# A planner driven by events, and nine pairs of heads kept on the chip, in a two-level attention kernel with an MLP behind it

## The chip, the cores and the metric

The kernel runs on one core of a Trainium2 chip. The metric is the device time of one execution in microseconds (us); the time before is the median of three runs. Five engines work side by side, each through its own list of instructions in order: TensorE (PE, with its weight loads as PEld), VectorE (DVE), ScalarE (ACT), GpSimd (POOL) and SyncE (SP, which here only issues DMAs). Engines wait for one another by semaphores. A DMA is issued by SP, ACT or POOL and carried out by 16 DMA engines that all queues share.

## The reference

Eight batches of eight heads, 576 tokens, head size 64. Each head's output is the sum of two attentions; the result goes through an MLP with 2048 hidden units.

```python
q_d, k_d, v_d = means of q, k, v over groups of 4 tokens       # 144 coarse tokens
out_up = repeat(softmax(q_d @ k_d.T / 8) @ v_d, 4)             # coarse attention
mask = abs(pos_i - pos_j) < 4                                  # a band of 7 keys
out_local = softmax(where(mask, q @ k.T / 8, -1e9)) @ v        # local attention
x = (out_up + out_local) as [8 * 576 tokens, 8 * 64]
h = x @ w_in;  result = (h * sigmoid(h)) @ w_out
```

## The kernel before, in words

**Attention** goes by pairs of heads, 32 of them; four pairs are one batch, that is 576 rows of `x`. For a pair `p` the steps are:

- `load_qk`, `load_v` and `load_vq` fetch q and k, v in overlapping windows of 64 tokens (rows of 256 bytes), and for pairs from `NVP` = 8 on v a second time in groups of four tokens. `cast`, `castw` and `castv` turn them to bf16, mostly on POOL; `castv` also adds the groups of four up (pooled v, tile `vd`).
- `T(p)`: 36 transposes of 64x64 by TensorE; `after_T` moves them out of PSUM (`qT`, `kT`) and adds up groups of four with two reductions on VectorE (`qd`, `kd`).
- `S(p)`: the scores, 20 local and 8 coarse matmuls into the banks `AB`; `after_S` takes two exponentials on ScalarE (`Pt`, `Pd`) and multiplies the local one by the 0/1 band on VectorE.
- `Z(p)`: the row sums by TensorE into columns of the banks `CD`; `after_Z` takes the reciprocal (`zr`). For `p < NDIR` = 4 it is split into three bf16 parts and spread over partitions by 15 matmuls (`RB`). For all others it goes to DRAM (`scr`) and comes back spread out (`Rb`): three DMAs on ACT's queue, the last two of which wait for the first to land.
- `PV(p)`: the products with v and pooled v, in `CD`; `after_PV` multiplies by `Rb` on VectorE (`xo`) and adds the coarse to the local part on POOL into `xT`, a ring of 1536 tokens.
- For pairs under 8 pooled v comes by 14 matmuls (`VP`) instead of `load_vq`.

From pair 6 on these steps are packed into visits: `V(n)` is PV of pair n-2, S of n, T of n+1 and Z of n-1, in one unit of TensorE.

**The MLP** goes by nine blocks of 512 tokens. `g1(j, f)` is four matmuls for 128 of the 2048 hidden units, `tanh` on ScalarE and one operation on VectorE into `gT`; the two banks `HP` take turns. `g2(j, tt, part)` is a quarter of 16 matmuls for 128 tokens of output; after the fourth quarter ScalarE evicts and SP stores. Block j can start when all pairs of its tokens are in `xT`: block 0 needs pairs 0 to 3, block 1 pairs 4 to 7.

**The order** is written out by hand for the units (`T0 T1 S0 T2 S1 Z0 RB0 ...`, then two or three `g1` after each step, and from visit 10 on four `g1` and four `g2` per visit). `Plan.order` then goes through each engine's units in a window (14 units on PE, 30 on POOL, 40 elsewhere) with assumed costs, and takes the first that is ready. DMAs are modelled by a ring per issuing engine. The eight weight loads, 1 MB of DRAM each, are given to POOL's queue at 10, 14, 18, 22, 34, 38, 42 and 46 us of planned time. Each engine runs its list in that order whatever the real times are.

Of the kernel before, what the change touches and what calls it, by code (L numbers as in the profile page):

```python
# [1 line left out]

# [16 lines left out]
NVP = 8  # L19
NDIR = 4  # L20


class Res:


    def __init__(self, name, psum=False):
        self.name, self.psum = name, psum
        self.writers, self.readers, self.prev = [], [], []
        self.last = {}
        self.dw, self.dr, self.prev2, self.dl = [], [], [], {}  # L30
# [11 lines left out]
class Prog:  # L42
# [23 lines left out]
    def op(self, eng, fn, r=(), w=(), dma=None):  # L66
# [4 lines left out]
        for x in r:  # L71
            if x.psum:
                deps += [(o, False) for e, o in x.last.items() if e != eng]
            else:
                deps += [(o, True) for o in x.writers]
        for x in w:
            if x.psum:
                deps += [(o, False) for e, o in x.last.items() if e != eng]
# [70 lines left out]
class Unit:  # L149


    __slots__ = ("eng", "name", "ops", "cost", "dcost", "prio", "idx", "pre", "succ", "npre",
                 "ready", "start", "end")

    def __init__(self, eng, name, cost, prio, dcost=0.0):
        self.eng, self.name, self.cost, self.prio, self.dcost = eng, name, cost, prio, dcost
        self.ops, self.pre, self.succ = [], set(), []
        self.ready = 0.0


class Plan:


    LAT = {"PE": 0.25, "ACT": 0.2, "DVE": 0.2, "POOL": 0.2, "SP": 0.1}

    def __init__(self):
        self.units = []

    def unit(self, eng, name, cost, prio=None, dcost=0.0):
        u = Unit(eng, name, cost, prio, dcost)  # L170
        u.idx = len(self.units)
        if u.prio is None:
            u.prio = u.idx
        self.units.append(u)
        return u

    def op(self, u, fn, r=(), w=(), dma=None):
        u.ops.append((fn, tuple(r), tuple(w), dma))
        pre = set()
        for x in r:  # L180
            if x.psum:
                pre.update(x.dw)
                pre.update(v for v in x.dr if v.eng != u.eng)
                x.dr.append(u)
            else:
                pre.update(x.dw)
        for x in w:
            if x.psum:
                pre.update(x.dw)
                pre.update(x.dr)  # L190
                if x.dr or not x.dw or x.dw[-1] is not u:
                    x.dr, x.dw = [], [u]
            else:
                if x.dr or x in r:
                    x.prev2 = x.dr + x.dw
                    x.dr, x.dw = [], []
                pre.update(x.prev2)
                pre.update(v for v in x.dw if v.eng != u.eng)
        for x in r:
            if not x.psum and x not in w:  # L200
                x.dr.append(u)
        for x in w:
            if not x.psum:
                x.dw.append(u)
        pre.discard(u)
        u.pre |= pre

    def order(self, look):
        free = {e: 0.0 for e in Prog.ENGS}
        ring = {e: 0.0 for e in Prog.ENGS}  # L210
        for u in self.units:
            u.pre = {v for v in u.pre}
            u.npre = len(u.pre)
            for v in u.pre:
                v.succ.append(u)
        pend = {e: [u for u in self.units if u.eng == e] for e in Prog.ENGS}
        head = {e: 0 for e in Prog.ENGS}
        taken = set()
        res = []
        left = len(self.units)  # L220
        while left:
            best = None
            for e in Prog.ENGS:
                lst = pend[e]
                while head[e] < len(lst) and lst[head[e]] in taken:
                    head[e] += 1
                win = [u for u in lst[head[e]:head[e] + look[e]] if u not in taken and not u.npre]
                if not win:
                    continue
                t = max(free[e], min(u.ready for u in win))  # L230
                c = min((u for u in win if u.ready <= t + 0.05), key=lambda u: (u.prio, u.idx))
                t = max(t, c.ready)
                if best is None or t < best[0]:
                    best = (t, c)
            t, u = best
            u.start = t
            free[u.eng] = t + u.cost
            if u.dcost:
                e = u.eng
                begin = max(t + u.cost + 0.4, ring[e])  # L240
                other = max(x for y, x in ring.items() if y != e)
                ring[e] = begin + u.dcost + min(u.dcost, max(0.0, other - begin))
                u.end = ring[e] + 1.6
                if e == "SP":
                    free[e] = max(free[e], ring[e] - 4.0)
            else:
                u.end = t + u.cost + self.LAT[u.eng]
            for v in u.succ:
                v.npre -= 1
                same = v.eng == u.eng and not u.dcost  # L250
                v.ready = max(v.ready, t + u.cost + (0.06 if u.eng != "PE" else 0.0) if same else u.end)
            taken.add(u)
            res.append(u)
            left -= 1
        res.sort(key=lambda u: u.start)
        return res


def bass_hourglass_attn__then__act_silu_kernel(
# [9 lines left out]
    with kctx:  # L269
        E = kctx.enter_context  # L270
        L = Plan()
# [7 lines left out]
        def sb(name, shape, dt, n=1):  # L279
            ts = [E(nc.sbuf_tensor(f"{name}{i}", shape, dt)) for i in range(n)]  # L280
            return ts if n > 1 else ts[0]

        NQK, NVS, NVQ, NB, NX, NT, NP_, NV, NR = 4, 4, 2, 3, 2, 2, 4, 4, 3
        w_in_sb = sb("w_in_sb", [128, 4, DFF], F32R)
        w_out_bf = sb("w_out_bf", [128, 16, 512], BF16)
        xT = sb("xT", [128, 4, XR], F32)
# [3 lines left out]

        qk = sb("qk", [128, 2, 576], F32, NQK)
        vs = sb("vs", [128, 10, 64], F32, NVS)
        vq = sb("vq", [128, 4, 256], F32, NVQ)
        vt = sb("vt", [128, 4, 128], F32)
        qkb = sb("qkb", [128, 2, 576], BF16, NB)
        vb = sb("vb", [128, 10, 64], BF16, NV)
        vd = sb("vd", [128, 4, 64], BF16, NV)
# [4 lines left out]
        Pt = sb("Pt", [128, 2, 288], BF16, NP_)  # L302
        Pd = sb("Pd", [128, 2, 216], BF16, NP_)
        zr = sb("zr", [128, 2, 72], F32, 2)
        Rb = sb("Rb", [128, 720], F32, NR)
        xo = sb("xo", [128, 2, 360], F32, NX)
        scr = [nc.dram_tensor(f"scr{i}", [128, 144], F32, kind="Internal").ap() for i in range(NR)]

        sel = gT[1][:, 0:2, :].rearrange("p a (y m) -> p (a y) m", m=128)[:, 0:5, :]
        selr = [R("g1_0"), R("g1_1")]  # L310
# [43 lines left out]
        def constants():  # L354
# [13 lines left out]
            for i in range(NT):  # L368
                for a, b in ((0, 3), (579, 592)):
                    zero(kT[i][:, a:b], f"kTp{i}{a}", cost=0.07)  # L370
# [561 lines left out]
```

## Time and profile before

| | |
|---|---|
| three runs | 392.88 us median, 388.90 to 393.71 |
| span of the profiled execution | 389.9 us (no other time of it is given) |
| busy: PE / DVE / ACT / POOL | 337.1 / 239.5 / 169.1 / 159.1 us |
| moved by DMA | 66.1 MB, 170 GB/s over the span |
| one `g1` matmul, one `g2` matmul (mean) | 430 ns x576, 380 ns x546 |
| reciprocal of 128x144 | 1056 ns x32 |

How to read it: matmuls are pipelined, so 430 ns is the length of one and four in a row take 0.92 us. A busy PE is not a fast PE: the row PEclk tells the granted clock in tenths. A group's line gives its tile out and in, the line of the source, the count, the busy time, and the idle time of the engine before it with what ended it. L339 is the helper that records every matmul and L426 the one that records every DMA, so these are told apart by tile.

### The profile page before, as it was taken

How to read it: one execution, taken by the hardware profiler on the slowest of the kernel's cores; microseconds unless marked ns; L12 is line 12 of the kernel's file. 1: busy time of each engine (PE TensorE's matmuls, PEld its weight loads, DVE VectorE, ACT ScalarE, POOL GpSimd, SP SyncE). 2: the span in 40 equal slices, each digit the busy share in tenths (PEclk: the TensorE clock that was granted, in tenths of full speed). 3: DMA queues.
4: the chain of work that ended last, by engine and by line, in shares of the span. 5: the costliest groups of instructions: out<-in, count | busy, mean ns of one | idle time of the engine just before them, and what ended most of it. 6: DMA issues, size and time to landing. Idle time of an engine off the chain costs nothing.

```text
span 389.9 us, 12145 instructions
## 1 busy us (share of the span) xinstructions
PE 337.1 (86%) x5262; PEld 219.8 (56%) x5292; DVE 239.5 (61%) x395; ACT 169.1 (43%) x296; POOL 159.1 (41%) x199
## 2 busy tenths in 40 slices
PE   2587497545699998999989999899999999999996
PEld 1365265434466665656656666566665556656642
DVE  6686456555678867667868688677676443344310
ACT  3643245323255445545545455354553334344321
POOL 7371643435846564655556466555311200000000
PEclk9998668985599999999999999999999999999999
DMA  6999999996968896897797878443222201001012
GB/s 185 283 332 310 224 272 239 230 249 136 270 185 221 216 241 188 208 261 205 208 262 189 229 209 203 129 115 104 77 101 74 74 27 54 29 27 54 29 54 81
DMA packets 79038, 66.12 MB, mean 170 GB/s; under 512 B 47242, under 2 KB 60554, under 8 KB 78986
## 3 DMA queue, kind: packets, MB, share of 16 engines
q1 hardware_dynamic: 66250, 46.68, 45.2%
q10 hardware_dynamic: 8512, 12.39, 12.2%
q0 software_dynamic: 4224, 6.29, 6.7%
q8 instruction: 41, 0.67, 0.7%
q14 instruction: 11, 0.09, 0.1%
HBM read 55.93 MB, written 11.50 MB: 173 GB/s over the span
## 4 chain that ended last, share of the span: by engine, by line
PE 68%; DMA 15%; SPq 6%; issue 3%; DVE 3%; ACTq 2%; ACT 2%; POOL 1%; POOLq 0%; DVEq 0%
PE HP L339 32%; PE o L339 21%; DMA scr<-zr 10%; PE pe_ L339 7%; SPq L426 6%; PE CD L339 5%; DMA vs<-in_v_dram 4%; ACTq L426 2%; PE AB L339 2%; DMA Rb<-scr 1%; DVE gT L754 1%; PE o L531 1%; PE pe_ L531 1%; DVE zr L673 1%; ACT th L752 1%
## 5 line engine op out<-in xcount | busy, mean ns | idle before, releaser
L339 PE MATMUL HP<-xT,w_in_sb 128*128 128x512 f32 x576 | 167.7, 430 | 8.9 <-DVE gT L754 4.6
L754 DVE SCALAR_TENSOR_TENSOR gT<-th,HP 128x512 bf16<-128x512 f32 x144 | 96.7, 685 | 114.4 <-ACT th L752 114.1
L339 PEld LDWEIGHTS HP<-xT,w_in_sb 128*128 128x128 f32 x576 | 109.7, 196 | 39.0 <-DVE gT L754 6.4
L752 ACT ACTIVATE th<-HP 128x512 f32<-128x512 f32 x144 | 85.8, 598 | 104.1 <-PE HP L339 85.7
L339 PE MATMUL o<-w_out_bf,gT 128*128 128x512 bf16 x437 | 102.2, 380 | 2.2 <-DVE qT L342 0.3
L339 PEld LDWEIGHTS o<-w_out_bf,gT 128*128 128x128 bf16 x464 | 42.2, 98 | 56.8 <-issue 6.4
L736 POOL TENSOR_TENSOR xT<-xo 128x576 fp32r<-128x576 f32 (+3 forms) x48 | 44.6, 941 | 57.3 <-DVE xo L709 57.3
L513 POOL CAST vb<-vs 128x640 bf16<-128x640 f32 x30 | 21.5, 717 | 73.6 <-PE CD L339 59.2
L769 ACT ACTIVATE osb<-o 128x512 f32<-128x512 f32 x29 | 17.3, 597 | 61.1 <-PE o L339 47.7
L673 DVE RECIPROCAL zr<-CD 128x144 f32<-128x144 f32 x32 | 33.8, 1056 | 8.3 <-PE CD L339 8.3
L503 POOL CAST qkb<-qk 128x1152 bf16<-128x1152 f32 x30 | 34.3, 1144 | 9.1 <-issue 5.7
L518 POOL TENSOR_TENSOR vt<-vq 128x512 f32<-128x512 f32 x24 | 30.5, 1271 | 8.5 <-DMA vq<-in_v_dram 8.5
L709 DVE TENSOR_TENSOR xo<-CD,Rb 128x720 f32<-128x720 f32 x32 | 28.7, 896 | 2.6 <-POOL xT L736 2.6
L541 ACT ACTIVATE kT<-pe_ 128x576 bf16<-128x576 bf16 x32 | 20.9, 653 | 17.0 <-PE pe_ L531 10.5
L531 PE MATMUL o<-idn,qkb 64*64 64x64 bf16 x576 | 17.5, 206 | 10.4 <-DVE qkb L498 5.6
L339 PE MATMUL CD<-Pd,vd 64*64 64x72 bf16 x384 | 16.1, 213 | 11.8 <-DVE vd L603 7.8
L339 PE MATMUL pe_<-w_out_bf,gT 128*128 128x512 bf16 x109 | 26.1, 380 | 0.2
L548 DVE TENSOR_REDUCE qd<-qT 128x144 bf16<-128x576 bf16 x32 | 23.8, 743 | 0.0
L545 DVE TENSOR_REDUCE kd<-kT 128x144 bf16<-128x576 bf16 x32 | 23.6, 738 | 0.0
L573 ACT ACTIVATE Pt<-AB 128x576 bf16<-128x576 f32 x32 | 20.7, 648 | 4.6 <-PE AB L339 4.6
L339 PEld LDWEIGHTS CD<-Pd,vd 64*64 64x64 bf16 x384 | 9.3, 112 | 22.6 <-issue 9.7
L531 PEld LDWEIGHTS o<-idn,qkb 64*64 64x64 bf16 x576 | 14.4, 120 | 11.2 <-DVE qkb L498 6.5
(62 smaller groups left out, 314.9 us busy)
## 6 DMA issues: line engine op xcount, KB each, us to landing
vs<-in_v_dram SPq DMA_DIRECT2D x126, 80.0 KB, 4.4
Rb<-scr ACTq DMA_DIRECT2D x56, 180.0 KB, 4.9
qk<-in_q_dram SPq DMA_DIRECT2D x32, 288.0 KB, 4.8
out_dram<-osb SPq DMA_DIRECT2D x36, 256.0 KB, 2.1
qk<-in_k_dram SPq DMA_DIRECT2D x31, 288.0 KB, 5.7
vq<-in_v_dram SPq DMA_DIRECT2D x24, 256.0 KB, 6.0
w_in_sb<-in_moe_w_in_dram POOLq DMA_DIRECT2D x4, 1024.0 KB, 10.0
w_out_bf<-in_moe_w_out_dram POOLq DMA_DIRECT2D x4, 512.0 KB, 9.2
```

Source lines behind the costliest of these rows:

```text
L339: L.op(u, lambda t: t.matmul(out_, lhsT, rhs, start=start, stop=stop, skip_group_check=True), r, w)
L426: return one(eng, name, cost, lambda s: s.dma_start(out_, in_), r, w, sem, prio, dcost)
L503: one("POOL", f"c{p}", 1.15, lambda g: g.tensor_copy(qkb[j][:, :, :], qk[i][:, :, :]), r=[R(f"qk{i}0"), R(f"qk{i}1")], w=[R(f"qkb{j}0"), R ...
L518: one("POOL", f"va{p}", 1.3, lambda g: g.tensor_tensor(vt[:, :, :], vq[i][:, :, 0:128], vq[i][:, :, 128:256], ALU.add), r=rr, w=[R("vt")])
L531: L.op(u, lambda e, o=o, w=w, j=j: e.transpose(o, w, idn[half(j), :]), [R("id"), R(f"qkb{n}{x}")], [rE if x else rF])
L545: one("DVE", f"mk{p}", 0.74, lambda e: e.tensor_reduce(kd[j][:, 0:SD], kT[j][:, 3:579].rearrange("p (g r) -> p g r", r=4), AX.X, ALU.add), ...
L548: one("DVE", f"mq{p}", 0.74, lambda e: e.tensor_reduce(qd[j][:, :], qT[j][:, :].rearrange("p (g r) -> p g r", r=4), AX.X, ALU.add), r=[R(f ...
L673: one("DVE", f"r{p}", 1.2, lambda e: e.reciprocal(zr[i][:, :, :], CD[:, :, 360:432]), r=rCD, w=[R(f"zr{i}")], prio=-4)
L709: one("DVE", f"m{p}", 0.92, lambda e: e.tensor_tensor(xo[x][:, :, :].rearrange("p x (m n) -> p x m n", n=72), CD[:, :, 0:360].rearrange("p ...
L736: one("POOL", f"a{p}", 0.15 + n * 0.0019, lambda g, dst=dst, in0=in0, in1=in1: g.tensor_tensor(dst, in0, in1, ALU.add), r=[R(f"xo{x}")], w ...
L752: one("ACT", f"t{j}_{f}", 0.62, lambda e: e.activation(th[tb][:, :], hps[hb], AF.Tanh, scale=0.5), r=[rH[hb]], w=[R(f"th{tb}")], prio=-1)
L754: one("DVE", f"s{j}_{f}", 0.71, lambda e: e.scalar_tensor_tensor(gT[j % 2][:, f, :], th[tb][:, :], 1.0, hps[hb], ALU.add, ALU.mult), r=[rH ...
```

## The change

Nearly all of the kernel body is rewritten; what is computed, the tiles' shapes and the sizes of the MLP stay.

- `Plan` gives way to `Sched`: tasks with a priority, resources taken from pools when a task starts and given back when its last user ends, and a simulation by events. The simulation lets all queues with DMAs in flight share the bandwidth. At each moment a free engine takes the ready task of highest priority: attention goes by pair, MLP units on TensorE after all attention.
- PSUM is two double banks `dd` (scores, products, spread reciprocals) and four single banks `sg` (transposes, pooled v, row sums, `g1`, `g2`), taken from the pools.
- Pairs 0 to 8 (`NS` = 9) are separate steps and stay on the chip: `RB` by 10 matmuls of 72 columns after two bf16 parts, pooled v by `VP` (pairs 0 to 9). For pairs 0 to 3 TensorE also makes the sums of four in `T` (36 more matmuls), and one exponential serves both scores; for pairs 0 to 7 the band is a bias that TensorE adds to the scores.
- From pair 9 on, visit n does PV of pair n-3 (was n-2). The DRAM round trip of the reciprocal is issued by SP instead of ACT.
- Row sums stand once per head on 128-row matmuls (14 instead of 28), and the reciprocal is 72 columns wide.
- The weight loads get 9, 12, 15, 18, 24, 28, 32 and 36 us as earliest planned times. Buffers are deeper: `qkb` 4, `vb`, `vd`, `Pt` 5, `qT`/`kT` 3.
- An operation of ACT, DVE or POOL on a PSUM bank now waits for the last operation of its own engine on that bank.

```diff
-NVP = 8
-NDIR = 4
+NS = 9
+SUM_PE = frozenset(range(0, 4))
+MASK_PE = frozenset(range(0, 8))
+RB_PE = frozenset(range(0, NS))
+VP_PE = frozenset(range(0, max(10, NS)))
...
-                deps += [(o, False) for e, o in x.last.items() if e != eng]
+                deps += [(o, e == eng and eng != "PE") for e, o in x.last.items()]
...
+                for t in sorted(ready[e], key=lambda t: (t.prio, t.idx)):
+                    if can(t):
+                        best = t
+                        break
...
+            L.task("PE", f"RB{p}", 0.6, prio, [f"rd{p}", made["sel"]], [("zp", p), ("rb", p)], rbm)
+            L.task("ACT", f"er{p}", 0.82, prio + 3, [f"RB{p}"], [("rb", p), ("Rb", p)], rbe)
...
-            eng = "ACT"
-            dma(eng, f"z{p}", scr[u][:, :], zf, [R(f"scr{u}")], f"scr{u}", 0.2, r=[R(f"zr{i}")], prio=-5)
+            dma("SP", f"z{p}", -3000 + p, [f"r{p}"], [("zr", p), ("Rb", p)], 0.25,
+                lambda: (scr[U("Rb", p)][:, :], zr[U("zr", p)][:, :]), lambda: f"scr{U('Rb', p)}",
+                lambda: [R(f"zr{U('zr', p)}")], lambda: [R(f"scr{U('Rb', p)}")])
...
+                dma("SP", f"b{p}_{h}", -3000 + p, [f"z{p}"], [("Rb", p)], 0.6, mk,
...
         def V(n):
-            pv = n - 2 if n - 2 < NPAIR else None
-            z = n - 1 if n - 1 < NPAIR else None
+            pv = n - 3 if NS <= n - 3 < NPAIR else None
+            z = n - 1 if NS <= n - 1 < NPAIR else None
+            s = n if NS <= n < NPAIR else None
+            t = n + 1 if NS <= n + 1 < NPAIR else None
...
-        for c, t in enumerate((10, 14, 18, 22, 34, 38, 42, 46)):
-            load_w(c).ready = float(t)
-        for name in "T0 T1 S0 T2 S1 Z0 RB0 VP0 T3 S2 Z1 PV0 RB1 VP1 S3 Z2 PV1 RB2 VP2 Z3 PV2 RB3 VP3 PV3".split():
+        for p in range(NS):
+            T(p, 10 * p)
+            S(p, 10 * p)
+            VP(p, 10 * p + 5)
+            Z(p, 10 * p)
+            PV(p, 10 * p)
+        for n in range(NS - 1, NPAIR + 3):
+            V(n)
...
+        for n, d in enumerate(done):
+            if d[0] == "g1":
+                g1(d[1], d[2], 1000 + n)
+            else:
+                g2(d[1], d[2], d[3], 1000 + n)
...
+W_GATES = (9.0, 12.0, 15.0, 18.0, 24.0, 28.0, 32.0, 36.0)
```

## The prediction

> **What bounds the kernel now.** I read the page's slices first, then busy times by stretch, then the chain of work that ended last, then the timelines of ScalarE, SP and TensorE. (Columns by stretch: length, busy time and instructions of each engine, clock, DMA share, GB/s.)
>
> ```profile
> PE   2587497545699998999989999899999999999996
> PEclk9998668985599999999999999999999999999999
> 0.00:47.30 47.30, 25.06 (x715) 19.29 (x715) 31.97 (x84) 18.74 (x33) 25.79 (x55) 0.91 1.04 266
> 47.30:103.00 55.70, 36.13 (x829) 27.10 (x829) 31.66 (x51) 18.71 (x34) 26.52 (x28) 0.71 1.03 229
> 103.00:300.00 197.00, 189.75 (x3317) 122.98 (x3332) 145.31 (x217) 99.42 (x175) 104.41 (x116) 0.99 0.68 185
> 300.00:390.00 90.00, 86.16 (x424) 50.48 (x417) 30.57 (x44) 32.28 (x54) 2.43 (x2) 1.00 0.13 49
> ```
>
> From 103 us on TensorE is full (96%) at full clock; before, it is not. The tile view of `w_in` counts 65 `g1` matmuls up to 103 us, 16 units and one matmul, and that of `w_out` no `g2`. So 128 `g1` units and all 144 `g2` units lie behind 103.1 us, where visit 10 ends. In the chain four `g1` matmuls take 0.92 us (8 in 1.84) and four `g2` 0.868 (16 in 3.47): 128 x 0.922 + 144 x 0.868 = 118.0 + 125.0 = 243.0 us. TensorE ends at 386.7, so the 24 visits in that stretch and all gaps took 283.6 - 243.0 = 40.6 us. A visit itself is 1.24 us in TensorE's timeline (138.09 to 139.33), 24 of them 29.8: only 10.8 us of gaps in 283.6. Time is to be had in the first 103 us or hardly at all. The chain and ScalarE's timeline show why they were slow:
>
> ```profile
> 39.20 5.01 DMA vs<-in_v_dram
> 44.41 0.61 issue
> 45.02 1.15 POOL qkb L503
> 46.16 1.18 POOL xT L736
> 47.38 2.50 PE HP L339 x5
> 53.77 5.69 DMA scr<-zr
> ...
> 78.19 6.23 DMA scr<-zr
> ...
> 73.29 1.36 ACTq L426 DMA_DIRECT2D Rb<-scr  x2
> 74.70 1.08 ACT L752 ACTIVATE th<-HP 128x512 f32<-128x512 f32 x2 [5.21 <-issue]
> ```
>
> Up to 47 us: `xT` of pairs 1 to 3 waits on POOL behind casts of v for later pairs, whose DMAs are late (VectorE had pair 3 done at 40.0, POOL added it at 46.1 to 47.3). From 53 to 103: the spread DMAs wait on ScalarE's queue for `scr` to land, and `tanh`, queued behind, keeps `g1`'s banks full.
>
> **The change, part by part.** I count until the same work is done (16 `g1`, pairs 0 to 8), then add the rest.
>
> *First MLP unit.* Pair 3's v was issued from 16.9 to 20.0 us and its cast began at 25.46 after waiting for it. The new order puts it ahead of pair 4's q and k (1.04 us earlier), but weights 0 to 2 go out at 9, 12 and 15 us of planned time rather than at the 11.4, 20.2 and 21.6 seen: 2 MB sooner, at the 300 to 400 GB/s of 18 to 36 us some 6 us at most. So v lands at 24 to 31. Then cast 0.72, `VP` (14 matmuls of half height 26.46 to 27.48, now 7 full: 0.5 to 1.0), eviction 0.29 x2 halves, `PV` 0.4, multiplication 0.90, add 1.21: 4.5 us with the hops. The engines allow it: per early pair VectorE and ScalarE have copies 0.69 + 0.65, two of about 0.3 for the sums of four, an exponential of 1.05 (0.65 + 0.53, one start less), a reciprocal between 0.53 and 1.06, four splitting steps of 0.22 to 0.31, `er` 0.8 (0.53 + 0.41 now), `xo` 0.90, `vd` 0.4, casts 0.92 and 0.74: 8 us, 32 for four pairs, over two engines 16, behind 4.6 us of loads and 4 of constants. So 29 to 35, up to 47.4 if POOL is again misordered; I take **34**, near the upper end, since lists made ahead meet late DMAs as in the lines above. POOL's constants cost less (20 selections of 15 columns from 5.10 to 11.46 shrink to some 14 of about 0.25).
>
> *To the same state.* 16 x 0.922 = 14.8 us; pairs 4 to 8 each a visit's work 1.24, `VP` 0.4 to 1.0, `RB` 0.4 to 0.7 (15 matmuls of 144 took 1.11; now 10 of 72, no row so narrow), mask 0.3 to 0.6 (4 x 144 columns at 0.074 to 0.15): 2.4, five times 12.0. Sum 26.8 at full clock. The clock was 0.71 in the old stretch: 26.8/0.71 would be +11; with no gap +0. I take **+7**, the old clock being the nearest row. State reached at 34 + 26.8 + 7 = 67.8 instead of 103.1: **35.3 us gained**.
>
> *Work that moves.* Sums, mask, `RB` and `VP` are counted above; they cover up VectorE operations (two reductions of 0.74 for four pairs, products of 0.55 for eight), which were no bound. The round trips of pairs 4 to 8 go (0.44 MB each by the issue sizes), and `load_vq` of pairs 8 and 9.
>
> *Steady visits.* The 28 matmuls of S, 36 transposes and 20 local products stay. Row sums and coarse products were 40 matmuls of 64 rows, four side by side, and are 18 of 128 rows, two side by side, and 4 of the old kind: ten turns of the array either way, 0 ± 0.2 us a visit. VectorE saves 0 to 0.5 us on the reciprocal. An engine's waits for itself (the second exponential for the first) lie beside TensorE's 7.2 us of MLP per visit; uncovered they would be 0.1 to 0.5 us a pair, the latter if an exponential of 0.53 no longer overlapped at all.
>
> The row for a change between tile shapes: eight `CD` matmuls and the change to full height took 0.19 us (139.14 to 139.33), four without a change 0.05 (138.09 to 138.14), so it is at most 0.09 us. [...]
>
> *Round trip on SP.* SP issues per pair, from its timeline: v 2.60, q 0.61, k 0.43, vq 1.41, store 0.40, and what ScalarE issued until now, 0.34 + 1.10: 6.9 us.
>
> ```profile
> 151.21 2.60 SPq L426 DMA_DIRECT2D vs<-in_v_dram  x4
> ...
> 155.12 1.57 SPq L426 DMA_DIRECT2D vq<-in_v_dram  x3
> 156.74 0.42 SPq L426 DMA_DIRECT2D out_dram<-osb  x1
> ...
> 140.58 0.34 ACTq L426 DMA_DIRECT2D scr<-zr  x1
> 145.42 1.11 ACTq L426 DMA_DIRECT2D Rb<-scr  x2
> ```
>
> The wait for `scr` to land (4.8 us here, 3.2 in the median) now stands ahead of later pairs' loads and of stores. By its waits SP stood for 93 of the 197 us from 103 to 300, on evictions and casts; four buffers of q and k lie ahead, and the products come a visit later. That covers it: cost 0, and without cover the price of the slower rival. ScalarE loses the same wait.
>
> *The order afterwards.* TensorE has MLP work whenever attention is not ready. It must not run out: `g1` of block 1 needs pairs 0 to 7 (7.3 MB) and weights of 8.4 MB; at the 191 GB/s of the first 10 us and 290 after, 15.7 MB are there at 58 us, while block 0's `g1` and `g2` and five pairs give TensorE 14.8 + 13.9 + 12 us from 34 on, to 75. Enough, narrowly. The 10.8 us of gaps may shrink or grow; I leave them.
>
> **Sum.** 389.9 - 35.3 = 354.6 us of span. The page gives the profiled execution no time but its span; the median of the runs is 3.0 above it. So 357.6, stated as **357**.
>
> One more reading of the clock. The row of stretches says 1.00 for 20 to 30 us, yet the pace was half:
>
> ```profile
> 24.38 2.15 PE L339 MATMUL HP<-gT 128*128 128x144 bf16 x14 [0.17 <-DVE gT L681]
> 35.82 1.11 PE L339 MATMUL HP<-gT 128*128 128x144 bf16 x15
> ```
>
> [...]
>
> **Rivals.**
>
> *The front stays as slow* (18%). POOL, SP and DMA meet the lists late again: `xT` of pair 3 at 47.4, and the old clock: 47.4 + 26.8 + 11 = 85, gain 18, so 372 + 3 = 375. For it: DMA is at share 1.0 from 10 to 90 us and the bytes that block 0 needs are the same. Against: casts of pairs under 4 may go to three engines, so POOL holds fewer.
>
> *All of it works* (17%). First unit at 30, no clock loss, half of the gaps gone: 389.9 - (103.1 - 56.8) - 5 = 338.6, so 342.
>
> *SP becomes the bound, slower than before* (12%). Nothing may stand between `scr` and its spreading, so the 4.8 us add in full, with the waits for evictions ahead of stores: 6.9 + 4.8 = 11.7 a pair at least. After pair 31 two blocks remain, 32 x 1.79 = 57.3 us, and 3.2 to the end. With nine pairs done at 70, 23 pairs at 11.7: 70 + 269 + 57.3 + 3.2 = 400, so 403. It decides from (389.9 - 60.5 - 70)/23 = 11.3 us a pair. Against: SP is half idle now, and loads of other pairs can go out while `scr` lands.
>
> *The change doesn't do what it says*: the planner's order on the old path, about 390; it would need `tanh` still waiting on DMA in the first nine pairs, and I give it within the front's share.
>
> **How the numbers follow.** Forecast 53%, its own range 347 to 366; all works 17%, slow front 18%, SP 12%. The range takes in the first three, 338 to 383; outside lie SP's 12% and the ends of two others, some 18% in all. About 2% is what a measurement of this kernel tells from no change; 385 is that line below. The slow front reaches past it in a third of its cases: faster 0.82, same 0.06, slower 0.12.
>
> **What would show it.** Right: first `xT` matmul of `g1` near 34 us, 16 units by 68, the clock row without fives and sixes after 45, no `tanh` waiting on a DMA, TensorE at 95% from 70 on, SP's waits for `scr` under 4 us. Wrong: gaps in TensorE between 70 and 250, behind transposes waiting for casts or visits waiting for `xo`; then either loads come late through SP or four single banks don't suffice for `g1`, `g2` and transposes at once.

## The result, and the profile after

The changed kernel takes 380.29 us (median of four, 378.15 to 381.22) against 391.2 us before on the same chip: a ratio of 0.970, 95% interval 0.9635 to 0.9765, so 3% faster where 9% was forecast. Executions more than 1.5% above the fastest of their kernel (in `e1` one of 360.18 us beside 354.03 to 358.48) are left out of ratios and intervals, here and below, so a ratio need not be the quotient of the medians beside it. The profiled execution has a span of 376.4 us, 13.5 less than that of before, and a time of 378.15.

The page of the changed kernel, its slices (each 9.4 us long):

```profile
PE   3765999999975979979999899499999999999996
PEclk9966999999998989999999999789999999999999
```

The old row had one slow start, up to slice 11, and was full behind it. The new one is full from slice 5 on, and then has holes: slices 12, 13, 15, 18 and 26 above all. The same by stretches (columns by stretch: length, busy time and instructions of each engine, clock, DMA share, GB/s):

```profile
47.30:100.00 52.70, 51.32 (x995) 36.02 (x990) 44.22 (x80) 34.22 (x61) 30.55 (x32) 1.00 0.84 212
100.00:140.00 40.00, 30.87 (x421) 19.25 (x426) 21.30 (x33) 13.51 (x25) 22.31 (x27) 0.91 0.83 231
140.00:300.00 160.00, 148.14 (x2284) 97.36 (x2301) 111.52 (x168) 76.23 (x134) 75.39 (x80) 0.98 0.58 164
300.00:376.40 76.40, 72.87 (x321) 41.52 (x326) 24.48 (x36) 28.09 (x47) 0.00 (x0) 1.00 0.11 42
```

TensorE is 97% busy from 47 to 100 us (65% from 47 to 103 before), then 77% for 40 us. The old kernel was 97% busy in those 40 us, at the same clock of 0.91:

```profile
100.00:140.00 40.00, 38.68 (x747) 26.06 (x752) 28.53 (x43) 19.43 (x34) 23.83 (x31) 0.91 0.83 219
```

To see what that is worth I counted TensorE's work rather than its busy time: each `g1` matmul at 0.2305 us and each `g2` matmul at 0.217 (the prediction's 0.922 and 0.868, divided by four; missing `g2` records made up in proportion), those of attention by their columns and the share of the array that they fill. For these it is an estimate: in the new kernel 10 matmuls of 72 columns on half of the array take 0.16 us (147.75 to 147.91), 0.162 by the count, and 20 of 58 columns on a quarter 0.18 (146.80 to 146.98), 0.13 by the count. That makes 293.7 us of work before and 299.4 after, for more of the pooled v and the spread reciprocals, the sums of four and the mask are now TensorE's. "Lost" is time less work.

| stretch, us | work before | lost before | work after | lost after |
|---|---|---|---|---|
| 0 to 100 | 29.2 | 70.8 | 62.3 | 37.7 |
| 100 to 300 | 177.9 | 22.1 | 163.3 | 36.7 |
| 300 to end | 86.5 | 3.4 | 73.8 | 2.6 |

At 100 us the new kernel has done 33 us more work, part of it new (5.7 in all). **It then gives 14.6 us back between 100 and 300 us.** Together 33.1 - 14.6 + 0.8 - 5.7 = 13.6, the difference of the spans but for rounding.

Where it is lost can be read in the chain of work that ended last (start, length, what):

```profile
101.92 1.15 POOL qkb L551
103.16 0.43 SPq L524
103.63 0.43 SPq L524
104.11 0.60 SPq L592
...
111.30 0.63 SPq L592
...
112.64 0.62 SPq L592
113.30 2.97 DMA scr<-zr
116.30 0.62 DVE zr L938
117.14 0.92 DVE xo L897
118.10 1.23 PE dd L401 x38
```

From 103.16 to 113.30 the chain runs through SP's issues one behind the other: nothing is being waited for but SP's own turn. SP's timeline for the same time (start, length, what):

```profile
103.16 0.43 SPq L524 DMA_DIRECT2D scr<-zr  x1
103.63 0.43 SPq L524 DMA_DIRECT2D qk<-in_k_dram  x1
104.11 2.60 SPq L592 DMA_DIRECT2D vs<-in_v_dram  x4
106.75 0.61 SPq L612 DMA_DIRECT2D vq<-in_v_dram  x1
107.40 0.93 SPq L615 DMA_DIRECT2D vq<-in_v_dram  x2
108.38 0.42 SPq L524 DMA_DIRECT2D qk<-in_q_dram  x1
108.84 0.43 SPq L524 DMA_DIRECT2D qk<-in_k_dram  x1
109.32 1.94 SPq L524 DMA_DIRECT2D Rb<-scr  x2
111.30 1.96 SPq L592 DMA_DIRECT2D vs<-in_v_dram  x3
113.30 0.61 SPq L524 DMA_DIRECT2D scr<-zr  x1
```

Each issue begins some 0.04 us after the one before it ended. The spreading of one pair (109.32) went out with 5.4 us of other pairs' loads between it and its `scr` of 103.16; the next `scr` follows 2 us of v loads. What stands still meanwhile is VectorE, and behind it TensorE (the last row):

```profile
105.88 0.61 DVE L938 RECIPROCAL zr<-dd 128x72 f32<-128x72 f32 x1 [3.47 <-DMA scr<-zr]
116.30 0.61 DVE L938 RECIPROCAL zr<-dd 128x72 f32<-128x72 f32 x1 [4.68 <-DMA scr<-zr]
124.47 0.91 DVE L897 TENSOR_TENSOR xo<-dd,Rb 128x720 f32<-128x720 f32 x1 [3.50 <-DMA Rb<-scr]
118.10 0.48 PE L401 MATMUL dd<-Pt,vb 64*64 64x58 bf16 x20 [3.72 <-DVE xo L897]
```

The loads are not late here: those of pair 11, the last that block 2 needs, had all been issued by 73.4 us (by 75.8 in `e1` below). Late is the round trip. Pair 10's reciprocal was ready at 94.1 us, its `scr` went out at 103.2, its spreading at 109.3, and its multiplication began at 117.1. SP's issues summed up in steps of 20 us:

| us | 80 | 100 | 120 | 140 | 160 | 180 | 200 | 220 | 240 |
|---|---|---|---|---|---|---|---|---|---|
| before, of 20 us | 13.4 | 12.6 | 13.6 | 11.8 | 15.5 | 14.4 | 13.3 | 12.2 | 8.5 |
| after, of 20 us | 18.8 | 18.7 | 18.6 | 17.9 | 18.6 | 15.5 | 18.7 | 14.7 | 4.8 |

From 80 to 180 us SP issues for 93% of the time. What is left are its waits, for ScalarE's output tiles (mostly one of 16.9 us), for `scr` and for reciprocals (waits of SP from 80 to 290 us: total, times, longest):

```profile
SPq L524 <- ACT osb L1057: 20.1, 5, 16.9
SPq L524 <- DMA scr<-zr: 16.4, 10, 3.1
SPq L524 <- DVE zr L938: 6.3, 4, 2.8
```

What the MLP feels is `xT`. Block 2 could start at 126.9 us, when pair 11's addition came (POOL, 125.46 to 127.18); blocks 3, 4 and 6 start with pairs 15, 19 and 27 at 168.4, 203.1 and 281.0 us, block 5 at 244.7, 5.6 us behind its pair 23, and block 7 at 301.6, 6.4 us behind pair 31. Pair 8's addition ends at 88.0 us and pair 31's at 295.2: 9.0 us a pair. (18 of these us lie between pairs 24 and 25, where the list has TensorE at the MLP; `e1` shows the same.) A pair's share of TensorE's work is 4.5 x (0.922 + 0.868) + 1.24 = 9.3 us. So attention, which has to run ahead of the MLP by a block (4.5 pairs), hardly gained on it, and TensorE stood still for 6.0 us before block 2, 1.8 before block 3 and 0.5 before block 4. A second loss at 238 us is a late store, which holds an output tile and through it `g2`'s bank (waits of TensorE, 100 to 290 us):

```profile
PE sg L401 <- ACT osb L1057: 5.4, 1, 5.4
PE dd L401 <- DVE xo L897: 4.2, 2, 3.7
```

### The profile page after: what moved, and what is told of

It reads as the page before. It is cut to its first block, busy times and chain, and to the rows that moved or that the text cites. A ratio compares the mean times of both kernels' runs of the same rounds, so it can differ in the third digit from the quotient of the medians.

```text
span 376.4 us, 11390 instructions
## 1 busy us (share of the span) xinstructions
PE 334.3 (89%) x4829; PEld 217.3 (58%) x4864; DVE 230.2 (61%) x418; ACT 176.2 (47%) x305; POOL 151.2 (40%) x177
## 4 chain that ended last, share of the span: by engine, by line
PE 60%; DMA 17%; SPq 9%; DVE 7%; issue 3%; ACT 3%; POOL 1%; DVEq 0%; POOLq 0%; ACTq 0%
PE sg L401 52%; DMA scr<-zr 8%; PE dd L401 6%; SPq L592 4%; SPq L524 4%; DMA qk<-in_k_dram 3%; DMA vs<-in_v_dram 3%; PE sg L657 2%; DMA Rb<-scr 2%; DVE gT L1027 2%; DVE xo L897 2%; DMA out_dram<-osb 1%; DVE zr L938 1%; SPq L615 1%; ACT th L1022 1%
## 5 line engine op out<-in xcount | busy, mean ns | idle before, releaser
L401 PE MATMUL sg<-xT,w_in_sb 128*128 128x512 f32 x576 | 158.5, 419 | 5.5 <-DVE gT L1027 4.5
L401 PE MATMUL sg<-w_out_bf,gT 128*128 128x512 bf16 x541 | 130.9, 383 | 9.2 <-ACT osb L1057 5.4
L1027 DVE SCALAR_TENSOR_TENSOR gT<-th,sg 128x512 bf16<-128x512 f32 x144 | 97.2, 682 | 54.6 <-ACT th L1022 52.9
L401 PEld LDWEIGHTS sg<-xT,w_in_sb 128*128 128x128 f32 x576 | 108.8, 193 | 35.7 <-DVE gT L1027 7.9
L1022 ACT ACTIVATE th<-sg 128x512 f32<-128x512 f32 x144 | 86.1, 598 | 91.8 <-PE sg L401 79.2
L401 PEld LDWEIGHTS sg<-w_out_bf,gT 128*128 128x128 bf16 x576 | 51.0, 98 | 72.1 <-issue 12.7
L1057 ACT ACTIVATE osb<-sg 128x512 f32<-128x512 f32 x36 | 21.6, 599 | 61.2 <-PE sg L401 40.1
L897 DVE TENSOR_TENSOR xo<-dd,Rb 128x720 f32<-128x720 f32 x32 | 29.0, 905 | 19.9 <-DMA Rb<-scr 9.6
L746 ACT ACTIVATE Pt<-dd 128x576 bf16<-128x576 f32 (+1 forms) x32 | 22.2, 693 | 21.9 <-PE dd L401 21.7
L409 DVE COPY qT<-sg 128x576 bf16<-128x576 bf16 x26 | 19.6, 756 | 20.7 <-PE sg L657 19.0
L657 PE MATMUL sg<-idf,qkb 64*64 64x64 bf16 x1152 | 17.4, 200 | 10.5 <-ACT qkb L405 6.4
L938 DVE RECIPROCAL zr<-dd 128x72 f32<-128x72 f32 x23 | 13.8, 601 | 19.6 <-DMA scr<-zr 17.6
L657 PEld LDWEIGHTS sg<-idf,qkb 64*64 64x64 bf16 x1152 | 14.0, 113 | 12.2 <-ACT qkb L405 6.7
L405 ACT ACTIVATE kT<-sg 128x576 bf16<-128x576 bf16 x28 | 18.3, 653 | 2.9 <-PE sg L657 2.5
## 6 DMA issues: line engine op xcount, KB each, us to landing
w_in_sb<-in_moe_w_in_dram POOLq DMA_DIRECT2D x4, 1024.0 KB, 10.4
```

What stands on the lines that cost most here:

```text
L401: P.op("PE", lambda t: t.matmul(out_, lhsT, rhs, start=start, stop=stop, skip_group_check=True), r, w)
L409: P.op(eng, lambda e: e.tensor_copy(out_, in_), r, w)
L657: P.op("PE", lambda e, o=o, w=w, j=j: e.transpose(o, w, idf[half(j), half(j)]), [R("idf"), R(f"qkb{n}{x}")], [rk])
L746: P.op("ACT", lambda e: e.activation(Pt[m][:, :, 0:w], dd[d][:, :, 0:w], AF.Exp, scale=0.125), rdd[d], [R(f"P{m}")] + ([R(f"Pd{m}")] if on ...
L897: P.op("DVE", lambda e: e.tensor_tensor(xo[x][:, :, :].rearrange("p x (m n) -> p x m n", n=72), dd[d][:, :, 0:360].rearrange("p x (m n) -> ...
L1022: P.op("ACT", lambda e: e.activation(th[i][:, :], sg[b][:, :], AF.Tanh, scale=0.5), [rsg[b]], [R(f"th{i}")])
```

## The experiments

The first theory, **issue time**: SP has too many DMAs to issue, so attention's pace is SP's. Its rivals: **waits**, the landing of `scr` that stands in SP's queue; **buffers** for the reciprocal; **bytes**, the 16 DMA engines; and **ScalarE**, that taking the round trip off it was the useful half of the change. Later came **order**: the lists were made with issue and landing times that the chip doesn't keep. In the expectations A is issue time, B waits, D bytes, E ScalarE and F order, where letters stand; C and G are explained where they first come. C, that PSUM banks, casts or the ring set the pace, falls with `e1`. All times are medians of four executions beside 390.4 to 391.8 us of before; `e12` has ten. "Last `xT`" is the start of the last addition on POOL (309.8 us before, 294.0 after).

| run | edit to the changed kernel | us | ratio to before, 95% | last `xT` |
|---|---|---|---|---|
| | none | 380.3 | 0.9635 to 0.9765 | 294.0 |
| e1 | round trip's three DMAs not issued | 356.6 | 0.9010 to 0.9173 | 269.0 |
| e2 | the same DMAs, from constants | 375.0 | 0.9503 to 0.9651 | 288.3 |
| e3 | stores issued by ACT | 367.6 | 0.9282 to 0.9460 | 283.1 |
| e4 | four reciprocal buffers | 377.8 | 0.9567 to 0.9740 | 296.1 |
| e5 | whole round trip on ACT | 367.6 | 0.9342 to 0.9529 | 285.5 |
| e6 | stores and `scr` on ACT | 361.3 | 0.9186 to 0.9376 | 278.5 |
| e8 | pooled v by TensorE for all pairs | 372.7 | 0.9458 to 0.9652 | 270.3 |
| e9 | e8 and e3 | 371.6 | 0.9450 to 0.9643 | 269.7 |
| e10 | e5 and e3 | 367.1 | 0.9353 to 0.9470 | 283.9 |
| e11 | planner told longer SP and landing times | 364.4 | 0.9287 to 0.9399 | 282.3 |
| e12 | `NS` = 4 | 391.3 | 1.0018 to 1.0121 | 302.2 |
| e13 | no sums of four, no mask by TensorE | 377.8 | 0.9584 to 0.9740 | 290.3 |
| e14 | e11 and e6 | **354.0** | 0.9007 to 0.9138 | 273.4 |
| e15 | only the landing time of e11 | 372.7 | 0.9469 to 0.9645 | 291.4 |
| e16 | planner told shorter SP times | 375.3 | 0.9518 to 0.9680 | 284.0 |
| e17 | only the SP times of e11 | 374.2 | 0.9476 to 0.9686 | 287.1 |

### The round trip: gone, or without its waits

```diff
             def go():
+                if name[0] == "z" or (name[0] == "b" and "_" in name):
+                    return
                 out_, in_ = mk()
```

> The planner's order is untouched, but the three DMAs of the round trip (one out, two back) are not issued for pairs 9 to 31, and the multiplication takes whatever stands in Rb: the normalisation of these pairs is left out. Theory A, SP's issuing is the bound of attention after pair 9 (18.6 of 20 us busy from 80 to 180): SP has 1.4 us less to issue per pair and nothing to wait for; the last pair's xT is there near 265 us instead of 295, TensorE's starved stretches (100 to 140, 240 to 260) close, and the time falls by 15 to 25 us to 355 to 365. Theory B, it is the latency of the trip that in-order SP and VectorE wait out: the same fall, since the latency goes too; the next kernel tells A from B. Theory C, attention is paced by PSUM banks, casts or the xT ring: within 4 us of the changed kernel's 380.

In `e2` the three DMAs stay, with the same sizes, but read a constant tile and a constant in DRAM, so that nothing has to land first:

```diff
             dma("SP", f"z{p}", ...
-                lambda: (scr[U("Rb", p)][:, :], zr[U("zr", p)][:, :]), ...
+                lambda: (scd[p][:, :], zc[:, :]), ...
...
-                    return Rb[u][half(h), :], bass.AP(tensor=scr[u].tensor, ...
+                    return Rb[u][half(h), :], bass.AP(tensor=scc.tensor, ...
```

> The same three DMAs of the same sizes are issued by SP at the same places, but they read constants, so that SP waits neither for the reciprocal nor for scr to land, and VectorE's reciprocal not for its buffer; the normalisation of pairs 9 to 31 is left out. Theory A (issue time): hardly faster than the changed kernel, 374 to 380, SP still 90% busy from 80 to 180. Theory B (waits): nearly all of the gain of the kernel without the trip, 355 to 367. Theory C: 376 to 380.

Without the trip 356.6 us, with the trip but without its waits 375.0. Of the 23.7 us that the trip costs, taking the waits alone returns 5.3, and the intervals of `e2` and of the changed kernel overlap a little. The stretches of `e1`:

```profile
100.00:140.00 40.00, 40.00 (x678) 25.94 (x677) 31.66 (x46) 21.42 (x38) 24.46 (x30) 1.00 0.83 232
140.00:300.00 160.00, 160.00 (x2265) 103.76 (x2263) 114.28 (x171) 80.54 (x140) 73.72 (x78) 1.00 0.37 109
```

and of `e2`:

```profile
100.00:140.00 40.00, 31.64 (x504) 19.40 (x491) 21.59 (x35) 14.72 (x26) 22.97 (x28) 0.91 0.85 231
```

With the trip's issues left out, TensorE has no idle time after 100 us, in the time in which the DMA share hardly differs (0.83 and 0.85). With them, waits or not, it stands for 8 of 40 us. In `e2` SP still issues for 18.4 to 18.8 of each 20 us from 80 to 180: the time of the waits was filled by the next issue. So SP's own waits lose to issue time. What `e2` doesn't take away is the trip's place in SP's list: VectorE still stood 14.7 us from 100 to 140 until the spread constants had come.

### Other buffers, other queues

`e4`, four reciprocal buffers instead of two:

```diff
+        zr += [E(nc.sbuf_tensor(f"zrx{i}", [128, 72], F32)) for i in range(2)]
...
-                d, i = L.unit[cd], U("zr", p)
+                d, i = L.unit[cd], p % 4
```

> Everything as in the changed kernel, but the reciprocals rotate through four buffers instead of two, so that VectorE's reciprocal no longer waits (17.6 us in 9 waits) for SP to have sent the one of two pairs before. Theory A: the wait moves on to the multiplication that needs Rb, 376 to 380. Theory B: 5 to 12 us faster, 368 to 375. Theory C: 380.

It can't be told from no edit, and the last `xT` is not earlier. The wait moved on: from 95 to 290 us VectorE no longer waits for `scr` (17.6 us with no edit), but 16.0 us for the spread reciprocals (8.5). `e3`, `e5`, `e6` and `e10` leave every DMA, its bytes and its place in the order, and change only the engine that issues it:

```diff
-                P.op(eng, lambda s: s.dma_start(out_, in_), r(), w(), sem())
+                e_ = "ACT" if name.startswith("out") else eng
+                P.op(e_, lambda s: s.dma_start(out_, in_), r(), w(), sem())
```

> Everything as in the changed kernel, but the 36 stores are issued by ScalarE at the place in its list that the plan gives them on SP's. SP loses 0.42 us per store and its waits for evictions (20 us between 80 and 290, one of 16.9); ScalarE gains the issue and, on it, stands right behind the eviction. Theory A: 4 to 10 us faster, 370 to 376. Theory B: the waits for scr stay, 376 to 380. Theory C: 380, or slower by 2 if ScalarE's 0.42 us per store delays tanh.

> The changed kernel with one part undone: the three DMAs of the round trip are issued by ScalarE, as before the change, at the places where the plan has them on SP's list; bytes and order are the same. SP has 1.44 us less to issue per pair, ScalarE has it and waits for scr to land ahead of tanh. Theory A (SP's issuing paces attention): faster than the changed kernel, 362 to 372, SP under 85% busy from 100 to 180, the last xT before 285 us; some of the gain is lost to tanh waiting. Rival D (bytes: the trip's 0.4 MB per pair compete with the loads): no change, 377 to 382. Rival E (moving it off ScalarE was right, its waits cost more than SP's): slower, 383 to 392.

> Stores and the first DMA of the trip (reciprocal to scr) are issued by ScalarE; the two that wait for scr to land stay on SP, so that ScalarE waits only for VectorE's reciprocal. SP has some 0.85 us less per pair than in the changed kernel, 0.43 less than with the stores alone moved (367.6). Theory A: 360 to 366. Rival D: as with the stores alone, 366 to 369. Rival E: 368 to 374, since ScalarE waits for reciprocals.

> All 36 stores and the whole round trip are issued by ScalarE, the order is the changed kernel's; SP only loads. Theory A alone: SP has 5.05 us per pair, the least of all kernels with the whole work, 355 to 361. With ScalarE's waits for scr weighed in (they were what the old kernel's tanh waited for): no better than stores and the first DMA moved (361.3), 361 to 368.

All four are faster than the changed kernel, by 13 to 19 us, with every byte still moved: bytes are out. So is ScalarE: with the whole trip back on ACT (`e5`) the kernel is not slower but 13 us faster than with it on SP. In `e5` SP issues for 12.8, 14.9 and 11.1 of each 20 us from 140 to 200, where it had 17.9, 18.6 and 15.5. Between the four I draw no line, as their intervals overlap; more moved is not visibly better (`e10` beside `e6`).

A third way to relieve SP is to drop a load. With pooled v by TensorE for all pairs, `load_vq` (1.55 us of issues a pair) is gone, for some 11 us more of TensorE's work, by the estimate in the expectation:

```diff
-VP_PE = frozenset(range(0, max(10, NS)))
+VP_PE = frozenset(range(0, NPAIR))
```

> Pooled v by TensorE for all pairs (VP_PE is all 32), the order planned anew: three loads fewer per pair on SP (1.41 us) and 0.33 MB, no pooled adds on POOL, but 22 more times 7 matmuls on TensorE and an eviction, some 0.5 us each or 11 us in all. The round trip is whole and on SP. Theory A: SP's relief is worth as much as without the trip (about 20 us), less the 11: 366 to 374. Theory B (latency of the trip): only the 11 us are seen, 385 to 392. Rival D: as A, since bytes go too.

> The same with the stores on ScalarE. Theory A: SP has 5.1 us to issue per pair and is no bound any more; what is left is TensorE's own work of some 310 us and the start: 358 to 368, not much below the kernel without the extra matmuls and the stores moved (367.6). Theory B: 370 to 380. Rival D: as with the stores on SP, less 2.

The last `xT` comes at 270.3 us, as early as without the round trip (269.0), and the kernel is 7.6 us faster despite the added work, though the intervals just overlap. With the stores off SP too (`e9`) nothing more is gained.

### Which part of the change made the start fast

```diff
-NS = 9
+NS = 4
```

> One part undone: only pairs 0 to 3 keep their reciprocals on the chip (NS = 4, as before the change), pairs 4 to 8 take visits and the round trip by SP, the order planned anew. Theory A: five more trips on SP in the stretch where it is full, and block 1's xT later than at 80 us: slower than the changed kernel by 8 to 20 us, 388 to 400. Rival G (the front's gain came from the start and the planner, not from the chip-side reciprocals): 376 to 384.

With pairs 4 to 8 packed into visits and their reciprocals sent through DRAM (the edit does both), the whole gain is gone: 391.3 us. The slices of `e12` show the old trough again, at 78 to 107 us (slices 9 to 11):

```profile
PE   2746999954599779998999899999999999999996
PEclk9956799985589988998999999999999999999999
```

`g1` of block 1 starts at 104.0 us, as it did before (103.0) and not at 80.7. The rest of the early edits are not needed for the gain:

```diff
-SUM_PE = frozenset(range(0, 4))
-MASK_PE = frozenset(range(0, 8))
+SUM_PE = frozenset()
+MASK_PE = frozenset()
```

> Another part undone: sums of four and the band are made by VectorE for all pairs, with two exponentials, as before the change (SUM_PE and MASK_PE empty), the order planned anew. The prediction held them for neutral: 377 to 384, the first g1 within 2 us of 37 us. If TensorE's extra work (5.7 us more than before by the count of its matmuls) counts: 373 to 377. If they start the MLP sooner: 384 to 390.

The first `g1` came 8 us later (45.9 us), which I had not expected, block 1 at 81.6, and the time is not to be told from no edit.

### The order of SP's list

The planner assumes 1.8 us from the end of a transfer to its landing being known, and 0.36 to 0.45 us for most issues of SP. In the trace `scr`, 36 KB, takes 3.5 us to land, and SP's issues last 0.42 to 0.62 us. `e11` puts those into the planner and moves no DMA to another engine:

```diff
-    LAND, BACKLOG = 1.8, 4.0
+    LAND, BACKLOG = 3.2, 4.0
...
+        if eng == "SP":
+            cost = {0.45: 0.62, 0.63: 0.66, 1.35: 1.55, 0.36: 0.45}.get(cost, cost)
```

> The changed kernel with only the planner's assumed costs of SP set nearer to what the trace shows (0.62 us for a load of q or k and for a DMA of the trip, 0.66 for v, 1.55 for three loads of pooled v, 0.45 for a store, 3.2 us to landing instead of 1.8); issuers stay. Theory A (SP cannot issue faster than 6.9 us a pair): 375 to 382. Rival F (SP has the time, but the order made with too short costs makes it wait): 362 to 372.

364.4 us, 16 us faster with the same DMAs on the same queue. SP is still full (18.3 to 18.7 of 20 us from 60 to 220), but its waits for `scr` are fewer and the gaps at 100 us smaller. Waits of SP from 80 to 290 us, then a stretch, in `e11`:

```profile
SPq L526 <- DMA scr<-zr: 7.6, 6, 3.5
```

```profile
100.00:140.00 40.00, 36.93 (x560) 23.37 (x552) 26.90 (x42) 18.90 (x33) 22.45 (x27) 1.00 0.80 226
```

So issue time is not the whole of it: with the same DMAs to issue, a list in another order brings `xT` 12 us sooner. Then both remedies together, each half of the second alone, and its opposite, all SP times times 0.8:

```diff
+        if eng == "SP":
+            cost = 0.8 * cost
```

> Truer SP costs in the planner (issue and landing, as in the run with 364.4) and stores and the trip's first DMA issued by ScalarE at the planned places (361.3 alone). One cause, SP late against its list: 358 to 364, little below either. Two causes: the gains of 16 and 19 us add up to 345 to 352.

> The changed kernel with only the planner's time to landing set to 3.2 us instead of 1.8. If the list's fault is that the trip's second half comes right after a landing assumed too early: most of the gain, 364 to 370. If it is SP's issue cost: 375 to 381.

> Only SP's issue costs set nearer to the trace in the planner (0.62, 0.66, 1.55, 0.45 us), landing left at 1.8. If the issue cost is the cause: 364 to 370, as with both. If the landing is: 375 to 381.

> The planner's SP costs 0.8 times those of the changed kernel, so still further from the trace (v 0.50 instead of 0.63 us, and so on). If the list built on an SP too fast is the cause: slower than the changed kernel, 382 to 392. If SP's capacity alone is: 377 to 382, since SP issues the same DMAs.

`e14` is the fastest complete kernel of the study: 354.0 us, 0.907 of before (0.9007 to 0.9138), and clearly below the changed kernel. Its slices and stretches:

```profile
PE   2766899999999999999999999999999999999996
PEclk9876699999999999999999999999999999999999
```

```profile
100.00:140.00 40.00, 40.00 (x678) 26.22 (x677) 31.82 (x47) 21.30 (x39) 24.02 (x29) 1.00 0.88 242
140.00:300.00 160.00, 160.00 (x2264) 103.73 (x2263) 113.56 (x170) 80.48 (x140) 73.49 (x78) 1.00 0.55 159
```

TensorE is never idle from 100 to 300 us. ScalarE carries the moved issues between its own operations (its timeline):

```profile
105.54 0.60 ACT L1060 ACTIVATE osb<-sg 128x512 f32<-128x512 f32 x1 [0.34 <-PE sg L403]
105.56 0.33 ACTq L527 DMA_DIRECT2D scr<-zr  x1
106.17 0.34 ACTq L527 DMA_DIRECT2D out_dram<-osb  x1
```

The two remedies give 19.0 (`e6`) and 15.9 us (`e11`) alone and 26.3 together: more than either, less than their sum of 34.9. The halves of `e11` give 7.6 and 6.1. **But `e16` falls against the theory of order:** shorter assumed times should have made a worse list (382 us or more), and it too was 5 us below the changed kernel, if at all (the intervals overlap). `e2`, `e15`, `e16` and `e17` all lie at 373 to 375 us and can't be told from one another. So a list made anew, for whatever reason, tends to come out a little below the changed kernel's, and only the two corrected assumptions together (`e11`) are clearly better. How much of the order's 16 us is a rule and how much is the luck of one list stays open. That relieving SP of issues helps stands on edits of different kinds, and most of them (`e1`, `e3`, `e5`, `e6`, `e10`) keep the changed kernel's own order.

How the two come together can be counted in the traces (all in us; "trip out" is the mean time, for pairs 9 to 14, from the end of the reciprocal until its spreading has been issued; VectorE's waits for the trip's DMAs are from 95 to 290 us):

| | none | e2 | e3 | e5 | e6 | e10 | e11 | e17 | e14 | e1 |
|---|---|---|---|---|---|---|---|---|---|---|
| time of the kernel | 380.3 | 375.0 | 367.6 | 367.6 | 361.3 | 367.1 | 364.4 | 374.2 | 354.0 | 356.6 |
| SP's issues a pair, 80 to 240 us | 7.5 | 7.6 | 7.2 | 6.1 | 6.8 | 5.8 | 7.6 | 7.4 | 6.8 | 6.0 |
| trip out | 14.9 | 17.4 | 12.3 | 9.1 | 13.0 | 8.6 | 8.8 | 6.7 | 6.2 | no trip |
| VectorE's waits for the trip | 26.1 | 16.8 | 18.7 | 2.5 | 11.1 | 6.2 | 15.2 | 13.9 | 0 | 0 |
| TensorE idle, 100 to 300 us | 21.0 | 14.8 | 10.1 | 13.1 | 9.8 | 10.4 | 5.7 | 13.4 | 0 | 0 |

No row orders all the runs: `e11` issues as long as no edit, and `e17` sends the trip out early and gains little. Nor is a full SP the fault by itself, for from 80 to 140 us it issues for 18.6 to 18.7 of each 20 us in `e1` too. But of these kernels the two in which VectorE never waits for the trip are the two without a hole. SP's list is fixed, and as long as SP is full, a DMA of the trip goes out late by all that stands before it; fewer issues on SP and a better place in the list both shorten that. In `e5` the longest hole left, 4.4 us, is a wait for stores to land.

## Why the prediction was right and wrong

**What bounds the kernel** held: nearly all that was won was won in the first 100 us, and the MLP's 243 us are as they were.

**First MLP unit**: predicted 34 us, bounds 29 to 47.4. The first `g1` matmul runs at 37.97 us, and pair 3's addition on POOL at 37.66 (it was 46.16 to 47.38). Pair 3's v landed at 28.8 us, within the 24 to 31 that I had taken, so late DMAs, my reason for leaning to the upper end, were not what came true. The chain behind v was mis-sized: 9.1 us where I had added up 4.5, for the pair's exponential, row sums, reciprocal and spreading came behind the cast of v and not beside it (from the chain of the changed kernel; `sg` L799 is the reciprocal, 34.99 the spreading and the products):

```profile
28.93 0.74 ACT vb L405
29.67 0.91 ACT Pt L746
33.13 0.63 DVE sg L799
34.99 1.51 PE dd L401 x32
```

**To the same state**: predicted 67.8 us. Taken as the moment at which as much work is left as at 103.1 us before, it was about 70 (36.0 us of work are needed, and they are done at 69.8). From 38 us on that is 31.8 us for some 25.3 of work by my count, so 6.5 lost, near the 7 that I had taken. The size came out; its reason did not, since the clock reads 1.00 from 47 us on (the stretch above) and work was done at less than full pace all the same. Two counts were off without much effect: 2.4 us for an early pair was the lowest sum of its own terms (2.34 to 3.54), and behind 103.1 us there are 23 visits, not 24. `e12` shows that the gain hangs on pairs 4 to 8 staying out of the visits and the round trip, and `e13` that the sums of four and the mask by TensorE pay for themselves and no more.

**Steady visits**: nothing speaks against 0. In `e14`, with the new visits, TensorE is full from 100 to 300 us and the kernel 3 us below the forecast. From 140 to 300 us my count of work leaves 8.5 us of that open, for 18 visits; for as many in the old kernel it leaves 16.3, of which 6.8 are idle time, so 9.5. So no sign of a hidden cost of the new visit; what a change between tile shapes costs (at most 0.09 us in the old timeline, 139.14 to 139.33) no run measures by itself.

**Round trip on SP: "cost 0, covered"** is the step that failed, and with it "the 10.8 us of gaps ... I leave them". From 69.8 us to the end the new kernel took 306.6 us where the old one took 286.8: 19.8 us, which is most of what is missing (33.3 gained instead of 35.3, then 19.8 lost instead of 0). The count of issues was near: 6.9 us a pair, and in the trace 141.7 us for the 19 pairs of 80 to 240 us, 7.5. What was wrong is the cover. I read SP as half idle from its waits in the old steady state. There SP waited for evictions and casts while TensorE, 96% busy at 9 us a pair, set the pace; I take the waits for a sign of that. The change starts block 1 of the MLP 22 us sooner (80.7 us against 103.0), and attention must then go faster than 9.3 us a pair until it is ahead again. It did 9.0. I had looked at the wait for `scr` as standing ahead of later pairs' loads; in the trace those loads stood ahead of the trip. From the end of pair 10's reciprocal to its multiplication 23.0 us went by, and products that come one visit (9 us) later, which was part of my cover, did not bridge that. In `e14` it was 15.5 us, and TensorE was full; so it was in `e1`, without a trip.

**The rival "SP becomes the bound"** had the place right and price and threshold wrong. Its condition, that nothing may stand between `scr` and its spreading, is the reverse of what the timeline shows. Its price was the 4.8 us wait, added in full to every pair; `e2` shows that waits are largely filled with other issues. Its threshold, 11.3 us a pair, was that for being slower than before. By the pace of `xT` the gain shrinks much sooner, as soon as attention can't outrun TensorE's 9.3.

**The slow front** would have given 375, close to the 380 measured, and is wrong all the same: the front was fast. `tanh` no longer waits for a DMA and the clock's row has no 5 or 6 after 45 us, as predicted. Of the signs that I named for being wrong, gaps between 70 and 250 us behind "visits waiting for `xo`" are what the profile shows (the 3.72 us at 118.10), but not for loads that come late through SP, as I had put it: it was the trip that came late. SP's waits for `scr` are 16.4 us, not under 4.

**The forecast's number** is about what the change gives when the trip comes in time: 357 us, against 354.0 in `e14`. The 3.0 us from span to time were too much: in the changed kernel it is 1.7 (376.4 and 378.15), and the rest was the difference between runs.

A single DMA of SP's takes 0.42 to 0.62 us to issue and 3.1 to 5.1 to land (medians of the kinds), so that one issue looks small beside it. That misleads here: thirteen issues a pair filled SP, and moving two kinds of them to ScalarE, with every byte still moved, was worth 19 us (`e6`).

## What to carry to other kernels

Idle time of an issuing queue in a profile is slack only at the pace of that profile: before adding work to it, divide its issue time per unit by the pace that the changed kernel needs while it catches up, not by the old one. Count issues, not bytes: here SP was full at 93% of the time in issues, with the DMA engines at a share of 0.83. Look which DMA in such a queue others wait for, because it goes out late by all that stands before it (15 us here); moving it, or some of the small DMAs before it, to an engine with idle time was the cheap remedy (13 to 19 us here). Where a list is made ahead from assumed costs, put the costs of a trace into it and look at more than one list: here the order alone was worth up to 16 us.

## What the runs showed of the hardware that I had not expected

The same DMA is issued faster by ScalarE than by a loaded SP. The tile view of `scr` in the changed kernel (min/median/max ns):

```profile
L524 SPq DMA_DIRECT2D scr<-zr x23: 320/584/2138, 87.7 to 286.3; - x23
```

and in `e14`, with ScalarE issuing it:

```profile
L527 ACTq DMA_DIRECT2D scr<-zr x23: 326/333/629, 85.5 to 264.1; - x23
```

333 ns against 584, at the same least of 320 to 326. On SP itself `scr` takes 350 and 320 ns where SP has stood idle before it (246.2 and 266.4 us), and mostly 580 to 620 between other issues. That points to the full queue and not to the engine; no run changes that alone.

Half the bytes brought nothing on the trip: `scr` with 36 KB takes 3.5 us to land (median), with 72 KB, from ScalarE's queue in the old kernel, it took 3.2. The reciprocal did gain: 601 ns for 72 columns, 1056 for 144.

Starving can cost twice. In some stretches in which TensorE waits, its granted clock falls too (changed kernel):

```profile
100.00:110.00 10.00, 7.45 (x132) 4.38 (x135) 5.81 (x10) 4.09 (x8) 5.53 (x7) 1.00 0.91 214
110.00:120.00 10.00, 5.95 (x125) 3.39 (x124) 5.09 (x9) 2.21 (x4) 6.58 (x10) 0.90 0.76 223
120.00:130.00 10.00, 9.84 (x141) 5.79 (x141) 5.91 (x10) 3.91 (x8) 6.62 (x9) 0.93 0.85 249
130.00:140.00 10.00, 7.63 (x27) 5.69 (x26) 4.49 (x7) 3.29 (x6) 3.58 (x3) 0.83 0.81 239
```

The clock is 0.90 and 0.83 in and just behind the gaps, and 1.00 from 100 us on in `e1` and `e14`, which have no gaps there. Behind the gap at 238 us it is 0.50 from 242 to 246 us and 0.79 from 246 to 250, and 12 `g1` matmuls take 4.51 us (from 244.68); at 1.00, from 249.72 on, 48 take 11.26, so 0.38 us each against 0.23. Not every gap does it: `e11` has 2.8 us of gaps from 120 to 140 us at a clock of 1.00.
